# The backward pass of an attention block with a gated MLP: TensorE in program order in the late stages, the w_down gradient among the dh tiles, a hold on the first O^T load, and moved query-stage loads

## The chip, the cores and the metric

The kernel runs on one core of a Trainium2 chip. The metric is the device time of one execution in microseconds (us), lower is better.

## The reference, cut to what matters

```python
def _fwd_reference(A_x, A_k_cache, A_v_cache, A_wq, A_wo, B_x, B_w_gate, B_w_up, B_w_down):
    xn = _layernorm(A_x)                     # [2048, 576], bf16
    s  = attention(xn, k_cache, v_cache, wq) @ wo     # 32 heads of 128, 2048 keys
    g  = silu((sigmoid(xn @ w_gate) * (xn @ w_up)) @ w_down)   # F = 4608
    return A_x + s * g
# the kernel gives this output and the gradients for x, K, V, wq, wo, w_gate, w_up, w_down
```

The order of work in the kernel: layer norm and gated MLP forward; then a long attention loop over 32 heads (to about 3530 us); then the *late stages* that this case is about. They are the O^T stage (attention's output times w_o, the gradient `doB` that enters the MLP, and its transpose `doBT`), 18 MLP blocks of 256 features (gradients of w_down, w_up, w_gate and their part of dx), and the query stage, 8 groups of 4 heads (gradients of w_q and w_o, the rest of dx, and the end of the layer-norm backward in groups 6 and 7). The attention loop writes O and dq to memory; the late stages read them back, and turn them by crossbar transposes (DMA_TRANSPOSE on the queue of SP). In what follows a *turn* is one such transpose, a *jam* is a stretch in which turns take several times their usual issue time, a *pair* is the two matmuls of 512 and 64 columns, dp is the matmul of dO with V^T in attention, and dST are the turned score gradients, sixteen slabs a head.

## The kernel before: the parts that the change and the argument touch

The accumulation of one weight-gradient tile over 16 row tiles, as pairs of matmuls of 512 and 64 columns:

```python
        def accumulate(acc, lhs, rhs, cols, dst):
            for st in range(NT):                       # NT = 16
                for n0, nn in ncs:                     # (0, 512), (512, 64)
                    nc.tensor.matmul(acc[:, n0:n0 + nn], lhsT=lhs[:, st, cols], rhs=rhs[:, st, n0:n0 + nn],
                                     start=(st == 0), stop=(st == NT - 1))
            alt.copy(dst[:, :D], acc[:, :D], eng="s")
```

One MLP block. `dh` has two PSUM buffers, `acc` three:

```python
                for st in range(0, NT, G2):            # G2 = 2: eight dh tiles
                    dh = ps.tile([P, G2, FB], f32, name="dh")
                    ...                                # 10 matmuls of 256 columns
                    nc.vector.tensor_tensor(du_blk[:, sp_, :], dh[:], a_blk[:, sp_, :], op=ALU.mult)
                    nc.scalar.mul(ndh[:], dh[:], -1.0)
                    nc.vector.tensor_tensor(dg_blk[:, sp_, :], ndh[:], nbl[:, sp_, :], op=ALU.mult)
                    if e % NTQ == 0:                   # after each half: crossbar turns of du and dg
                        for k in range(2):
                            turn_rows(dugT[k], dug[k], e - NTQ, e, FBT)
                ...
                if fb == NFB - 1:
                    nc.gpsimd.dma_start(ds_all, rows_view(ds_d, 0, D))    # 2.3 MB
                for fl in range(FBT):                  # w_down gradient, 2 x 16 pairs
                    dwd = outp.tile([P, D], bf, name="dwd")
                    accumulate(psa.tile(...), h_blk, doB, slice(fl * P, (fl + 1) * P), dwd)
                    nc.gpsimd.dma_start(out_8[r0:r0 + P, :], dwd[:])
                ...                                    # w_up, w_gate: 4 x 16 pairs
                for st in range(NT):                   # dx rows: 16 x 4 pairs, need duT and dgT
                    dx_row(acc, st, ...)
```

The late stages are traced in program order for SP, Pool and VectorE; TensorE and ScalarE are ordered by the compiler's scheduler. In the attention loop all engines are. The query stage loads each group's data at the group before (`load_on`, `load_dq`), turns dq (`dqbT`), and in group 6 also turns half of group 7's dq (`dqbT2`), so that rows can be finished there.

## Time and profile before

Three runs before the change gave a median of 4979.05 us (4975.73 to 4979.33). How to read: "start us, us, engine, line, operation, out<-in, count", and in brackets the idle time just before on that engine and what ended it. In lines of SPq the second number is issue time, for which the queue is held. The stages, as differences of first-matmul starts in TensorE's timeline:

| stage | from | us |
|---|---|---|
| attention's end: last head's first dp to first O^T matmul | 3463.86 | 69.4 |
| O^T stage, to the first dh | 3533.30 | 148.7 |
| MLP block 0 | 3681.99 | 49.1 |
| MLP blocks 1 to 16 | 3731.11 | 788.9 |
| MLP block 17 | 4520.01 | 56.2 |
| query group 0 | 4576.18 | 53.6 |
| groups 1 to 5 | 4629.76 | 235.2 |
| group 6 | 4864.96 | 64.6 |
| group 7 to the end of the span | 4929.58 | 51.7 |

VectorE's timeline of the kernel before in one MLP block shows the chain behind a dh tile: du, a wait for ScalarE's ndh, dg, and only then the next du. Its period is 1.75 us.

```profile
3781.71 0.69 DVE L1101 TENSOR_TENSOR du_blk<-dh,ah 128x512 bf16<-128x512 f32 x1 [0.34 <-PE dh L1098]
3783.12 0.43 DVE L1104 TENSOR_TENSOR dg_blk<-ndh,nbl 128x512 bf16<-128x512 bf16 x1 [0.72 <-ACT ndh L1103]
3783.47 0.68 DVE L1101 TENSOR_TENSOR du_blk<-dh,ah 128x512 bf16<-128x512 f32 x1
```

TensorE's timeline has two more waits, in query groups 0 and 6:

```profile
4612.41 17.51 PE L1052 MATMUL acc<-wdT,dqbT 128*128 128x512 bf16 x126 [4.71 <-ACT dqT L40]
...
4886.69 2.10 PE L1052 MATMUL acc<-wqT,dqbT 128*128 128x512 bf16 x8 [4.90 <-DMA dqbT<-dqb]
```

The first is a jam of crossbar turns: ScalarE's copy waits for the turn of an older one. The second is the turn of `dqbT2`, which the first finished row needs.

### The profile page before, as it was taken

The numbers are of one execution on the slowest core, as the hardware profiler recorded it, in microseconds if no ns is written. First come the engines' busy times: TensorE is split into PE (matmuls) and PEld (weight loads), VectorE is DVE, ScalarE is ACT, GpSimd is POOL, SyncE is SP. The second block draws the span as 40 slices with busy tenths as digits, with TensorE's granted clock in tenths as the row PEclk, the third lists the DMA queues.
The fourth block names the chain that finished last, engine by engine and source line by source line (L and its number), as shares of the span: only waits on it lengthen the run. The fifth ranks groups of instructions, "written<-read, shape, count | busy, mean of one in ns | idle before, by whom it ended". The sixth has DMA issues, their size and how long they took to land.

```text
span 4981.3 us, 100870 instructions
## 1 busy us (share of the span) xinstructions
PE 4857.5 (98%) x40276; PEld 2897.3 (58%) x41029; DVE 2790.1 (56%) x6554; ACT 2473.1 (50%) x4228; POOL 840.7 (17%) x1330
## 2 busy tenths in 40 slices
PE   9999999999999999999999999999899999999998
PEld 4445666666666666666666666665455555555454
DVE  4544665666666566566566666666334545453225
ACT  4422766766766766666676676676221111111111
POOL 3322111111111111111111111111221111111111
PEclk9999999999999999999999999999999999999999
DMA  7887999999999999999999999999999999998765
GB/s 260 273 204 173 224 229 225 226 233 228 225 229 221 229 227 225 228 232 230 224 225 237 222 231 226 230 225 224 206 224 235 230 212 228 214 222 160 207 167 146
DMA packets 3048180, 1097.68 MB, mean 220 GB/s; under 512 B 2951889, under 2 KB 2956114, under 8 KB 3047698
## 3 DMA queue, kind: packets, MB, share of 16 engines
q1 hardware_dynamic: 2948930, 771.66, 82.5%
q0 software_dynamic: 98160, 318.85, 20.3%
q8 instruction: 322, 5.28, 0.4%
q14 instruction: 160, 1.31, 0.1%
q10 hardware_dynamic: 608, 0.59, 0.0%
HBM read 175.31 MB, written 177.93 MB: 71 GB/s over the span
## 4 chain that ended last, share of the span: by engine, by line
PE 88%; DVE 4%; issue 3%; DMA 3%; ACT 2%; SPq 1%; POOL 0%; ACTq 0%; POOLq 0%; DVEq 0%
PE acc L683 18%; PE acc L744 17%; PE acc L997 11%; PE sp L636 8%; PE dp L706 8%; PE acc L1052 8%; PE acc L215 6%; PE u_ps L450 3%; PE g_ps L448 3%; PE acc L533 3%; PE acc L957 2%; DVE du_blk L1101 1%; ACT ndh L1103 1%; PE acct L145 1%; DMA dST<-Pq 1%
## 5 line engine op out<-in xcount | busy, mean ns | idle before, releaser
L654 ACT ACTIVATE Pq<-sp 128x1024 bf16<-128x1024 f32 x1024 | 1046.9, 1023 | 262.3 <-PE sp L636 219.2
L709 DVE SCALAR_TENSOR_TENSOR Pq<-dp,negdelta,Pq 128x1024 bf16<-128x1024 f32 x512 | 654.8, 1279 | 46.8 <-PE dp L706 46.6
L712 ACT ACTIVATE t<-dp,negdelta 128x1024 bf16<-128x1024 f32 x512 | 567.1, 1114 | 214.9 <-PE dp L706 165.0
L683 PEld LDWEIGHTS <-dST 128*128 128x128 bf16 x8192 | 508.3, 98 | 157.4 <-DMA dST<-Pq 16.9
L706 PE MATMUL dp<-VT,dOT 128*128 128x512 bf16 x1919 | 581.6, 379 | 2.3
L683 PEld LDWEIGHTS <-PT 128*128 128x128 bf16 x8192 | 500.1, 98 | 128.7 <-DMA PT<-Pq 8.6
L683 PE MATMUL acc<-Kn,dST 128*128 128x128 bf16 x8192 | 557.5, 219 | 13.6 <-DMA dST<-Pq 11.7
L636 PE MATMUL sp<-KQ 128*128 128x512 bf16 x1858 | 567.8, 379 | 2.2 <-ACT Pq L654 2.1
L683 PE MATMUL acc<-Vn,PT 128*128 128x128 bf16 x8192 | 542.1, 219 | 6.4 <-DMA PT<-Pq 4.4
L744 PE MATMUL acc<-Pq,dOn 128*128 128x512 bf16 x1983 | 527.8, 379 | 10.2 <-issue 0.2
L713 DVE TENSOR_TENSOR Pq<-t,Pq 128x1024 bf16<-128x1024 bf16 x512 | 354.4, 692 | 321.1 <-ACT t L712 306.3
L744 PE MATMUL acc<-Pq,Qn 128*128 128x512 bf16 x2013 | 523.7, 379 | 4.9
L1142 DVE TENSOR_TENSOR dxn<-acc,dxn 128x576 f32<-128x576 f32 x272 | 206.0, 757 | 316.9 <-PE acc L1052 316.9
L724 ACT ACTIVATE dq_n<-acc,rsc 128x128 bf16<-128x128 f32 x512 | 187.5, 366 | 339.4 <-PE acc L683 317.9
L744 PEld LDWEIGHTS <-Qn 128*128 128x128 bf16 x2048 | 200.3, 98 | 240.9 <-issue 1.6
L744 PEld LDWEIGHTS <-dOn 128*128 128x128 bf16 x2048 | 199.0, 98 | 234.6 <-issue 1.3
L1103 ACT ACTIVATE ndh<-dh 128x512 bf16<-128x512 f32 x144 | 86.0, 597 | 420.0 <-DVE du_blk L1101 419.9
L636 PEld LDWEIGHTS <-KQ 128*128 128x128 bf16 x2048 | 179.0, 98 | 123.8 <-issue 3.1
L706 PEld LDWEIGHTS <-dOT 128*128 128x128 bf16 x2048 | 178.8, 98 | 124.1 <-issue 11.7
L641 DVE TENSOR_REDUCE rs_all<-rsp 128x1 f32<-128x2 f32 x512 | 78.4, 153 | 306.5 <-ACT Pq L654 295.3
L677 POOL DMA_DIRECT2D on_d<-o_n x128 | 97.1, 759 | 778.7 <-DVE junk L695 458.9
L677 POOL DMA_DIRECT2D dq_d<-dq_n x128 | 97.9, 765 | 721.8 <-ACT dq_n L724 682.0
(209 smaller groups left out, 6800.1 us busy)
## 6 DMA issues: line engine op xcount, KB each, us to landing
out_dram<-kvn POOLq DMA_DIRECT2D x64, 512.0 KB, 3.9
ah<-a_d POOLq DMA_DIRECT2D x18, 1024.0 KB, 9.0
ah<-h_d POOLq DMA_DIRECT2D x18, 1024.0 KB, 10.8
h_d<-h_row POOLq DMA_DIRECT2D x64, 256.0 KB, 3.5
a_d<-a_row POOLq DMA_DIRECT2D x64, 256.0 KB, 3.8
x_all<-in_A_k_cache_dram SPq DMA_DIRECT2D x64, 256.0 KB, 3.8
on_d<-o_n POOLq DMA_DIRECT2D x128, 128.0 KB, 4.6
kvT_d<-KQ POOLq DMA_DIRECT2D x32, 512.0 KB, 5.4
```

Of the source, the lines that this page charges most:

```text
L215: nc.tensor.matmul(av[:, :CH], lhsT=w[:, i, :], rhs=srcT[:, i, cs], start=(i == 0), stop=(i == DT - 1))
L636: nc.tensor.matmul(sp[:, c * CH:(c + 1) * CH], lhsT=hs.QT[:, qt * P:(qt + 1) * P], rhs=hs.KT[:, hf * HW_ + c * CH: hf * HW_ + (c + 1) * CH ...
L654: nc.scalar.activation(Pq[:, hsl], sp[:], AF.Exp, scale=SCALE, accum_out=hs.rsp[:, hf:hf + 1])
L683: nc.tensor.matmul(hs.acc[:, 0, :], lhsT=T[:, kt, :], rhs=rhs[:, kt, :], start=(kt == 0), stop=(kt == NT - 1))
L706: nc.tensor.matmul(dp[:, c * CH:(c + 1) * CH], lhsT=hs.dOT[:, qt * P:(qt + 1) * P], rhs=hs.VT[:, hf * HW_ + c * CH: hf * HW_ + (c + 1) * C ...
L709: nc.vector.scalar_tensor_tensor(Pq[:, hsl], dp[:], hs.negdelta[:, qt:qt + 1], Pq[:, hsl], op0=ALU.add, op1=ALU.mult)
L712: nc.scalar.activation(t[:], dp[:], AF.Identity, bias=hs.negdelta[:, qt:qt + 1], scale=1.0)
L713: nc.vector.tensor_tensor(Pq[:, hsl], t[:], Pq[:, hsl], op=ALU.mult)
L744: nc.tensor.matmul(self.acc, lhsT=self.nat[:, qt, :], rhs=self.slabs[qt][:, cs], start=(qt == self.lo), stop=(qt == self.hi - 1))
L997: nc.tensor.matmul(acc[:, n0:n0 + nn], lhsT=lhs[:, st, cols], rhs=rhs[:, st, n0:n0 + nn], start=(st == 0), stop=(st == NT - 1))
L1052: nc.tensor.matmul(acc[:, n0:n0 + nn], lhsT=lT, rhs=w[:, n0:n0 + nn], start=(k == 0), stop=(k == len(terms) - 1))
L1142: nc.vector.tensor_tensor(dxn[:, st, :], acc[:, :D], dxn[:, st, :], op=ALU.add)
```

## The change

Its intent: (1) TensorE too follows program order in the late stages, and the w_down gradient's 32 pairs are written into the dh loop, four after each dh tile; (2) the first O^T load, 1 MB through the crossbar, is held back by a one-element copy that reads the fifteenth score-gradient slab, so that it can't stand among that head's turns; (3) in the query stage a group's data are loaded two groups ahead, right after the last use of the buffer, the turn of `dqbT2` moves behind the second head of group 6, and the finished rows begin after 5 steps instead of 4.

```diff
-            put(bl + NT, 0, lambda: load_oT(oTs[0], 0))
+            def first_oT():
+                g = max(0, NT - 2)
+                nc.gpsimd.tensor_copy(oTs[0][0:1, 0, 0:1], heads[H - 1].slabs[g][0:1, 0:1])
+                load_oT(oTs[0], 0)
+            put(bl + NT, 0, first_oT)
@@ late stages
-            tc.manual_schedule(engines={... SP, ... Pool, ... DVE}):
+            tc.manual_schedule(engines={... SP, ... Pool, ... DVE, ... PE}):
@@ MLP block
+                def dwd_unit():            # one row tile (a pair); store after the sixteenth
+                    ...
                     nc.vector.tensor_tensor(dg_blk[:, sp_, :], ndh[:], nbl[:, sp_, :], op=ALU.mult)
+                    for _ in range(FBT * G2):          # 4
+                        dwd_unit()
...
-                for fl in range(FBT):
-                    ... accumulate(...); store
+                while dwd_units:
+                    dwd_unit()
@@ query stage
+            if NHG > 1:
+                load_on(onqs[1][0], 1)
+                load_dq(onqs[1][1], 1)
...
-                if not final:
-                    load_on(onqs[(hg + 1) % 2][0], hg + 1)
-                    load_dq(onqs[(hg + 1) % 2][1], hg + 1)
...
-                if early:
-                    nc.sync.dma_start_transpose(wqT2[:], A_wq[:, (hg + 1) * HC:(hg + 2) * HC])
-                    turn_rows(dqbT2, onqs[(hg + 1) % 2][1], 0, NTE, HG)
...
-                wait_n = min(4 if early else 2, nsteps - 2)
+                wait_n = min(5 if early else 2, nsteps - 2)
...                                                    # in the head loop, after the head's dwq turn
+                    if early and hl == min(1, HG - 1):
+                        nc.sync.dma_start_transpose(wqT2[:], ...); turn_rows(dqbT2, ...)
...                                                    # after the head loop
+                    if hg + 2 < NHG:
+                        load_on(onb, hg + 2)
+                        load_dq(dqb, hg + 2)
```

More of the change, by code (lines that the diff above doesn't have):

```diff
@@ L882 @@
     with late("pc") as pc, late("pcf") as pcf, \
-            tc.manual_schedule(engines={mybir.EngineType.SP, mybir.EngineType.Pool, mybir.EngineType.DVE}):
+            tc.manual_schedule(engines={mybir.EngineType.SP, mybir.EngineType.Pool, mybir.EngineType.DVE, mybir.EngineType.PE}):
         xn_all = pc.tile([P, NT, D], bf, name="xn_all")
@@ L992, with accumulate @@
         px.release()
-        def accumulate(acc, lhs, rhs, cols, dst):
-            for st in range(NT):
+        def accumulate(acc, lhs, rhs, cols, dst, a=0, b=NT):
+            for st in range(a, b):
                 for n0, nn in ncs:
@@ L998, in accumulate @@
                                      start=(st == 0), stop=(st == NT - 1))
-            alt.copy(dst[:, :D], acc[:, :D], eng="s")
+            if b == NT:
+                alt.copy(dst[:, :D], acc[:, :D], eng="s")
         def store_T(out_, cols, stg_):
@@ L1089 @@
                 du_blk, dg_blk = dug
+                dwd_units = [(fl, st) for fl in range(FBT) for st in range(NT)]
+                dwd_box = []
+                def dwd_unit():
+                    fl, st = dwd_units.pop(0)
+                    if st == 0:
+                        dwd_box[:] = [outp.tile([P, D], bf, name="dwd"), psa.tile([P, WD], f32, name="acc", tag="acc")]
+                    accumulate(dwd_box[1], h_blk, doB, slice(fl * P, (fl + 1) * P), dwd_box[0], st, st + 1)
+                    if st == NT - 1:
+                        r0 = fb * FB + fl * P
+                        nc.gpsimd.dma_start(out_8[r0:r0 + P, :], dwd_box[0][:])
                 for st in range(0, NT, G2):
@@ L1115 @@
                     nc.gpsimd.dma_start(ds_all, rows_view(ds_d, 0, D))
-                for fl in range(FBT):
-                    dwd = outp.tile([P, D], bf, name="dwd")
-                    accumulate(psa.tile([P, WD], f32, name="acc", tag="acc"), h_blk, doB, slice(fl * P, (fl + 1) * P), dwd)
-                    r0 = fb * FB + fl * P
-                    nc.gpsimd.dma_start(out_8[r0:r0 + P, :], dwd[:])
+                while dwd_units:
+                    dwd_unit()
                 if fb == NFB - 1:
@@ L1227 @@
                     nc.sync.dma_start_transpose(dwq[:, :, lcols], dqTs[h % 2][:])
+                    if early and hl == min(1, HG - 1):
+                        nc.sync.dma_start_transpose(wqT2[:], A_wq[:, (hg + 1) * HC:(hg + 2) * HC])
+                        turn_rows(dqbT2, onqs[(hg + 1) % 2][1], 0, NTE, HG)
                     if final and hl == HG - 1:
```

## The prediction

> **What bounds the kernel now.** I read the page first, then the busy time by 100 us windows from the end of attention on, then TensorE's timeline at every dip, and last the SP queue's timeline and the chain of waits there. The change touches nothing before about 3500 us but one load, so only the last third can move.
>
> ```profile
> PE 4857.5 (98%) x40276; PEld 2897.3 (58%) x41029; DVE 2790.1 (56%) x6554; ACT 2473.1 (50%) x4228; POOL 840.7 (17%) x1330
> ```
> ```profile
> 3400.00:3500.00 100.00, 94.44 (x822) 59.32 (x835) 60.53 (x161) 63.80 (x110) 17.70 (x34) 0.98 1.14 223
> 3500.00:3600.00 100.00, 79.08 (x640) 44.04 (x652) 25.42 (x35) 16.61 (x33) 22.00 (x40) 0.91 0.94 199
> ...
> 3900.00:4000.00 100.00, 98.39 (x800) 56.89 (x813) 50.44 (x80) 17.29 (x29) 16.49 (x24) 1.00 0.95 221
> ...
> 4500.00:4600.00 100.00, 94.60 (x746) 51.56 (x759) 32.52 (x48) 12.32 (x20) 13.60 (x19) 0.97 0.88 166
> 4600.00:4700.00 100.00, 94.50 (x750) 48.67 (x764) 24.23 (x32) 10.65 (x17) 11.70 (x16) 0.98 0.82 204
> 4700.00:4800.00 100.00, 99.17 (x801) 51.45 (x816) 24.24 (x32) 11.48 (x18) 12.23 (x17) 1.00 0.61 177
> 4800.00:4900.00 100.00, 94.15 (x738) 48.64 (x752) 32.09 (x51) 10.56 (x16) 13.83 (x20) 0.97 0.72 196
> ```
> The first figure after the window's length is PE. TensorE is the bound nearly everywhere. From 3500 us it is idle for 67 us in all (1481 us of windows less 1414 us busy), and a part of that is the unavoidable tail. The change keeps every matmul, so its gain is a part of those 67 us plus idle time that busy time hides (some 20 us, below): under 2% of 4979 even if all of it went.
>
> Hidden idle time is in the MLP blocks (18 of them, 3682 to 4576 us). TensorE's timeline in one:
> ```profile
> 3780.42 2.35 PE L1098 MATMUL dh<-wdT,doBT 128*128 128x256 bf16 x20
> 3782.60 0.41 PE L997 MATMUL acc<-doB,ah 128*128 128x512 bf16 x2
> 3783.14 1.25 PE L1098 MATMUL dh<-wdT,doBT 128*128 128x256 bf16 x10
> 3784.23 0.62 PE L997 MATMUL acc<-doB,ah 128*128 128x512 bf16 x3
> 3784.89 1.25 PE L1098 MATMUL dh<-wdT,doBT 128*128 128x256 bf16 x10
> ...
> 3793.19 5.34 PE L997 MATMUL acc<-doB,ah 128*128 128x64 bf16 x43
> 3798.36 8.00 PE L997 MATMUL acc<-xn_all,du_blk 128*128 128x512 bf16 x62
> 3806.20 8.00 PE L997 MATMUL acc<-xn_all,dg_blk 128*128 128x512 bf16 x63
> ```
> So the scheduler already puts some w_down-gradient matmuls (doB, ah) between dh tiles, but only one or two pairs each, and two thirds of them stand in a lump after the last dh. dh tiles start every 1.75 us although a tile and two pairs need less: the next tile waits for its PSUM buffer.
>
> The two places where the crossbar queue stops TensorE, SP's queue first (issue time), then TensorE with its wait:
> ```profile
> 3502.77 4.93 SPq L584 DMA_TRANSPOSE KQ<-on_d  x1
> 3507.79 18.95 SPq L630 DMA_TRANSPOSE dST<-Pq  x8
> ```
> ```profile
> 3513.11 1.57 PE L683 MATMUL acc<-Kn,dST 128*128 128x128 bf16 x16 [4.02 <-DMA dST<-Pq]
> ...
> 4563.72 0.66 PE L1052 MATMUL acc<-wug,duT 128*128 128x512 bf16 x4 [2.08 <-DMA duT<-du_blk]
> 4566.56 0.74 PE L1052 MATMUL acc<-wug,dgT 128*128 128x64 bf16 x3 [2.18 <-DMA dgT<-dg_blk]
> ```
> The O^T load (KQ) holds SP for 4.93 us in the middle of sixteen score-gradient turns; the ninth comes late and TensorE waits 4.02 us. In the last MLP block the second half of dgT comes 25.6 us after its issue.
>
> **What the Trainium skill says.** (1) "TensorE: Matmul & The Clock Gate", section "Wait — 56ns, not 53.3ns?": back-to-back warm matmuls start N/2.4 GHz plus about 2.5 ns apart. That makes 109.2 ns for 256 columns and 215.8 + 29.2 = 245 ns for a 512 and 64 pair. The trace agrees: ten dh matmuls in 1.09 us (3783.14 to 3784.23), 32 pairs in 7.84 us (3798.36 to 3806.20). (2) Same page, "What's actually happening": after an idle window the clock is halved for some 3.4 us. The trace agrees: after the 4566 wait the four-matmul steps start 0.96 us apart for about 4.8 us, then 0.49. (3) "Perfetto Trace Analysis", "Tensor Engine Instruction": the end of a matmul is estimated. So I go by starts, not by busy time; it is why a 49.3 us block shows under 1 us idle.
>
> **The change, part by part.**
>
> (a) w_down gradient among dh, blocks 1 to 16. Floor of a block: 80 dh matmuls x 0.1092 = 8.7 us; w_down, w_up, w_gate gradients 32 pairs each and dx 64 pairs, 160 x 0.245 = 39.2 us; sum 47.9. Period now: (4520.01 - 3780.42) / 15 = 49.31. Loss 1.4 us. Its cause is the chain behind dh: VectorE du 0.68, ScalarE ndh 0.60, VectorE dg 0.42 and hand-overs, 1.75 us a tile, which is just the pitch seen. The change puts four pairs after each tile: 1.09 + 0.98 = 2.07 us of TensorE work, above 1.75, so the PSUM wait should be gone. All 32 pairs are then used up, so no lump. What follows (w_up) has du ready except the last slice, and 4 pairs stand between. Gain 1.4 x 16 = 22 us. TensorE in program order by itself costs nothing here, since the order seen is the program's but for these pairs.
>
> (b) Block 0. There VectorE also makes nbl (0.6), pitch about 2.35 us. Now the scheduler fills with up to four pairs and even w_up's. In program order 2.07 us of work meets 2.35: eight tiles lose up to 0.28 each. Loss about 1.5 us against now (49.1 us).
>
> (c) Block 17. It takes 4576.18 - 4520.01 = 56.2 us, 8.3 above the floor: 1.4 as in (a), 4.3 the two waits, about 2.4 the cold clock (five steps of 0.96 for 0.49). Cause: the 2.3 MB ds load is issued at 4532.93, just after the last dh and just before the second-half turns (4534.27 and 4540.47). In the change the Pool queue meets the two w_down-gradient stores first, and the second comes only when all dh and pairs are done plus the 0.64 copy: about 17.5 us into the block, estimate from the times above. The du turn is then issued at about 16.3 and the dg turn at 17 to 18, at or ahead of the ds load instead of behind. They are needed at 16.4 + 15.7 + 7.8 = 40 us. I expect both waits to go; 7 of 8.3 us, with one of doubt.
>
> (d) First O^T load. SP's turns take about 2.4 us each (18.95 / 8) and 4.93 go to O^T. Taking it out brings turns 9 to 16 forward by 4.9, so the 4.02 wait goes and with it about 2 us of cold clock. Against: if the queue places the load before the last turn, that turn is no earlier than now; and the load now arrives later. It is wanted when O^T matmuls begin (3533.3), and even then those take 6 us and TensorE then idles 10.5 us for w_o rows, which follow Pool's stores at the end of attention; so a late landing up to some 10 us costs nothing. The chain behind moves with attention's end. Gain 5 us, between 0 and 7.
>
> (e) Query stage. Eight groups; groups 1 to 5 start 47.04 us apart, exactly 192 pairs x 0.245, so nothing to gain. Group 0 loses 4.7 us and cold clock behind crossbar turns of 32.6 us issue time beside 4 MB of loads; the same loads are issued at about the same place: 0, plus or minus 4. Group 6 (4864.96 to 4929.58, 64.6 us) loses 4.9 us at the dqbT2 turn, which lands 21.7 us after the start. The change moves that turn behind the second head's: about 12.4 (third step plus copy), two short turns, w_q 2.2, then 6.8 as now: 24 us, for a row that begins at 19.6 + 1. The wait becomes some 3.5, but VectorE's rows (4.36 us each, 8 rows, 34.9) start at 25 instead of 24 and are what ends last: 25 + 35 + 8 x 0.69 = 65.8. So 0, plus or minus 2. The earlier loads for the group after next gain nothing: Pool already ran ahead and issued them at 4852.7. The last group keeps its 52 us.
>
> Sum: 22 - 1.5 + 7 + 5 + 0 = 32.5. Predicted 4979 - 32 = 4947 us.
>
> **Rivals.** R1: the pitch of dh isn't set by the chain to be overtaken, or four pairs make a new wait (the accumulator's copy on ScalarE between ndh, or later dg turns reaching dx late). For it: the slack between last dg and its use shrinks from about 27 to 23 us, DMA is 0.95 busy. Against: turns land in 4.0 us median in these blocks. Then (a) gives nothing: about 4967. R2: program order costs more than it saves where the scheduler filled (block 0, first O^T rows, group 6): some 10 us back, about 4957. R3: (c) moves the DMA jam instead of removing it: ds, on and the next loads, 2 MB each, then collide with the group 0 turns, which lengthen 4.7 to 10; about 4953. R4: everything works and group 0 and 6 give 3 to 5 each: 4938.
>
> **Range and chances.** (a) is counted sixteen times and rests on starts, so most weight lies within 10 us of 4947. The rivals are mostly on the slow side: 4937 to 4962. Faster by 2% would need 100 us, more than all idle time in these stages; slower by 2% would need 5 us a block everywhere. 0.01, 0.98, 0.01.
>
> **What would show it.** Period of dh starts 47.9 to 48.2 in blocks 1 to 16, dh tiles 2.07 us apart with eight other matmuls between; block 0 about 50.5; block 17 about 49 with no wait for dgT; no 4 us dST wait before the last O^T load and its issue after at least the fifteenth turn; group 6 at 63 to 67 us. A period still at 49.3 would make the prediction wrong, as would a new wait at dx rows 8 to 15 or an O^T load that lands after the w_o rows.

## The result, and the profile after

The changed kernel took 4962.84 us in the median of 4 runs (4958.1 to 4968.66), against 4977.39 for the kernel before (4 runs, 4973.89 to 4979.33). A ratio here is the mean time of one kernel's fast runs over that of the other's of the same rounds, so not quite the ratio of the medians that are quoted: 0.9972, 95% interval 0.9955 to 0.9989. That is a gain of 14.5 us by the medians where 32 were forecast; 4962.84 lies just above the range of 4937 to 4962.

TensorE's line of the changed kernel's page, then its busy time by 100 us windows (after the window's length: PE, PEld, DVE, ACT, POOL; then clock, DMA share, GB/s):

```profile
PE 4881.5 (98%) x41029; PEld 2895.9 (58%) x41029; DVE 2801.3 (56%) x6554; ACT 2474.6 (50%) x4228; POOL 842.3 (17%) x1331
```
```profile
3500.00:3600.00 100.00, 73.58 (x614) 42.77 (x613) 27.89 (x35) 19.99 (x36) 19.23 (x35) 0.86 0.93 187
...
3900.00:4000.00 100.00, 100.00 (x838) 58.95 (x837) 54.07 (x84) 18.50 (x32) 17.09 (x25) 1.00 1.04 224
...
4500.00:4600.00 100.00, 100.00 (x827) 54.76 (x826) 36.97 (x53) 13.51 (x22) 17.00 (x23) 1.00 0.76 202
4600.00:4700.00 100.00, 100.00 (x818) 51.41 (x817) 28.81 (x39) 10.22 (x16) 11.68 (x16) 1.00 0.69 200
...
4800.00:4900.00 100.00, 95.07 (x755) 48.40 (x754) 32.89 (x67) 15.04 (x22) 14.76 (x25) 0.97 0.65 159
```

The MLP blocks and the first query groups are now full. The hole in front of them, at 3500 to 3600 us, is 26 us here and was 21 in the first profile of before, but the stages begin 11 us later here, so the window does not hold the same work. (Some TensorE records were missing in the trace of before, 40276 of 41029; so the busy time of the page is not a fair comparison, and starts are.)

One MLP block in TensorE's timeline:

```profile
3747.71 1.26 PE L1115 MATMUL dh<-wdT,doBT 128*128 128x256 bf16 x10
3748.81 1.14 PE L1002 MATMUL acc<-doB,ah 128*128 128x512 bf16 x8
3749.79 1.26 PE L1115 MATMUL dh<-wdT,doBT 128*128 128x256 bf16 x10
...
3762.22 1.26 PE L1115 MATMUL dh<-wdT,doBT 128*128 128x256 bf16 x10
3763.31 1.14 PE L1002 MATMUL acc<-doB,ah 128*128 128x512 bf16 x8
3764.29 6.01 PE L1002 MATMUL acc<-xn_all,du_blk 128*128 128x512 bf16 x47
```

dh tiles start 2.07 us apart with eight other matmuls between, and nothing waits. Now the end of attention and the start of the O^T stage, SP's queue and then TensorE:

```profile
3486.68 39.47 SPq L630 DMA_TRANSPOSE dST<-Pq  x14
3526.32 5.12 SPq L584 DMA_TRANSPOSE KQ<-on_d  x1
3531.53 4.23 SPq L630 DMA_TRANSPOSE dST<-Pq  x2
3551.39 5.00 SPq L584 DMA_TRANSPOSE xnT<-on_d  x1
```
```profile
3536.00 1.89 PE L683 MATMUL acc<-Kn,dST 128*128 128x128 bf16 x16 [5.41 <-DMA dST<-Pq]
...
3570.12 6.87 PE L962 MATMUL acc<-dsT,xnT 128*128 128x512 bf16 x34 [19.47 <-DMA xnT<-on_d]
```

The O^T load now stands in front of the last two turns instead of in the middle of sixteen, and the wait went with it: 5.41 us at the fifteenth turn where it had been 4.02 at the ninth. The last line shows a larger one, which no edit here was aimed at: in the O^T stage TensorE waits for the second O^T load or for rows of w_o, 19.47 us at a stretch in this profile, 7.5 to 21.1 in the longest such wait of each of the fourteen. And group 6, SP's queue and then TensorE:

```profile
4848.90 9.14 SPq L1053 DMA_TRANSPOSE dqbT<-ah  x4
4858.27 2.52 SPq L1240 DMA_TRANSPOSE dwq<-dqT  x2
4860.83 3.26 SPq L1242 DMA_TRANSPOSE wqT<-in_A_wq_dram  x1
4864.20 4.24 SPq L1053 DMA_TRANSPOSE dqbT<-dqb  x1
```
```profile
4870.49 2.10 PE L1058 MATMUL acc<-wqT,dqbT 128*128 128x512 bf16 x8 [4.93 <-DMA dqbT<-dqb]
...
4908.34 6.52 PE L1058 MATMUL acc<-wdT,dqbT 128*128 128x512 bf16 x32 [3.21 <-DVE dxn L1261]
```

The group begins at 4844.82. Its first row still waits 4.93 us for `dqbT2`, which now comes 25.7 us after the start instead of 21.7; VectorE's rows follow from there, and TensorE waits for them again at the end (1.34 and 3.21 us). The first ten or so of its last sixteen pairs then start 480 ns apart instead of 245, so that four rows of 4 pairs take 6.4 us where they take 3.92 at full clock.

All stages, with the later profiles of both kernels (experiments below), in us:

| stage | before, three profiles | changed, two profiles |
|---|---|---|
| the last head's first dp starts at | 3463.9, 3465.7, 3463.8 | 3473.2, 3466.6 |
| attention's end | 69.4, 65.5, 72.6 | 71.1, 68.9 |
| O^T stage | 148.7, 153.8, 155.1 | 153.3, 153.8 |
| block 0 | 49.1, 49.1, 49.1 | 50.1, 50.1 |
| blocks 1 to 16 | 788.9, 789.0, 789.1 | 766.9, 766.9 |
| block 17 | 56.2, 52.2, 49.3 | 47.9, 47.9 |
| group 0 | 53.6, 47.0, 47.0 | 47.0, 47.0 |
| groups 1 to 5 | 235.2 in all | 235.2 in both |
| group 6 | 64.6, 64.2, 64.1 | 69.9, 67.9 |
| group 7 to the end | 51.7, 51.9, 51.9 | 52.2, 52.1 |

Two kinds of rows: MLP blocks 0 to 16 and groups 1 to 5 repeat to 0.2 us, attention's end, the O^T stage, block 17 and group 0 vary by 6 to 7 us in the three profiles of before. The first profile of before had the worst jam of the three.

### The profile page after: what moved, and what is told of

It reads as the page before. It is cut to its first block, busy times and chain, and to the rows that moved or that the text cites. A ratio compares the mean times of both kernels' runs of the same rounds, so it can differ in the third digit from the quotient of the medians.

```text
span 4966.9 us, 101629 instructions
## 1 busy us (share of the span) xinstructions
PE 4881.5 (98%) x41029; PEld 2895.9 (58%) x41029; DVE 2801.3 (56%) x6554; ACT 2474.6 (50%) x4228; POOL 842.3 (17%) x1331
## 5 line engine op out<-in xcount | busy, mean ns | idle before, releaser
L706 PE MATMUL dp<-VT,dOT 128*128 128x512 bf16 x2048 | 609.7, 379 | 2.2
L636 PE MATMUL sp<-KQ 128*128 128x512 bf16 x2048 | 609.5, 379 | 2.2 <-ACT Pq L654 2.1
```

The costliest lines, as they stand in the source:

```text
L636: nc.tensor.matmul(sp[:, c * CH:(c + 1) * CH], lhsT=hs.QT[:, qt * P:(qt + 1) * P], rhs=hs.KT[:, hf * HW_ + c * CH: hf * HW_ + (c + 1) * CH ...
L706: nc.tensor.matmul(dp[:, c * CH:(c + 1) * CH], lhsT=hs.dOT[:, qt * P:(qt + 1) * P], rhs=hs.VT[:, hf * HW_ + c * CH: hf * HW_ + (c + 1) * C ...
```

## The experiments

Twelve kernels ran, in three calls on three chips (1, 11 and 12; for the first result the record names no chip), so ratios of one call compare best. Runs of the kernel before had medians of 4978.20, 4977.49 and 4978.16 us and spread from 4960 to 4986. All gave a correct result. The stages of the ones that follow, in us, from TensorE's timeline as above:

| run | median us | ratio to before, 95% interval | attention's end | O^T | block 17 | group 0 | group 6 |
|---|---|---|---|---|---|---|---|
| e1_same (changed, again) | 4955.93 | 0.9958 (0.994 to 0.9977) | 68.9 | 153.8 | 47.9 | 47.0 | 67.9 |
| e2_no_hold | 4954.42 | 0.9957 (0.9937 to 0.9976) | 66.4 | 147.2 | 47.9 | 47.0 | 70.5 |
| e3_hold_only | 4976.61 | 1.0003 (0.9986 to 1.0021) | 68.0 | 146.2 | 53.0 | 47.0 | 63.5 |
| e4_old_query | 4950.94 | 0.9951 (0.9933 to 0.9969) | 66.8 | 148.4 | 47.9 | 55.2 | 62.9 |
| e5_order_only | 5028.58 | 1.0093 (1.0071 to 1.0115) | 71.3 | 152.4 | 51.8 | 47.0 | 64.6 |
| e7_ds_late | 4975.47 | 0.9987 (0.9969 to 1.0005) | 67.0 | 154.9 | 49.3 | 47.0 | 64.4 |
| e9_hold_last | 4955.95 | 0.9945 (0.9921 to 0.9969) | 64.4 | 142.7 | 47.9 | 47.0 | 69.5 |
| e6_among_only | 4956.02 | 0.9955 (0.9942 to 0.9968) | 62.2 | 150.3 | 48.2 | 54.9 | 63.2 |
| e10_early_turn | 4949.65 | 0.9944 (0.993 to 0.9958) | 65.6 | 153.9 | 48.2 | 46.8 | 56.6 |
| e11_both | 4941.82 | 0.9926 (0.9913 to 0.994) | 63.8 | 151.8 | 47.9 | 47.0 | 56.7 |

### How far one profile repeats: the two kernels again

No edit in either. The changed kernel:

> The changed kernel unedited, for a second profile. In the first pair of profiles the last head's first dp matmul came at 3473.2 us against 3463.9 before, although the instruction order up to there is the same. Theory A (run to run noise of the attention loop): that start moves by some 5 us or more either way in this profile, and the stages from the first O^T matmul on repeat to within 2 us: O^T stage 153, MLP blocks 1 to 16 767, block 17 48, group 0 47.0, group 6 70 us. Theory B (the change slows attention itself): dp starts again at 3473 or later. Gain over before 14 us in either.

The kernel before, two more times:

> The kernel before, unedited, profiled a second time. Theory A (the first profile of before fell on a bad jam): block 17 plus group 0 take clearly less than the 109.7 us of the first profile, near the 100.0 that the hold-only run showed with the same code there. Theory B (the jam is the same each run): 109 to 110. Blocks 1 to 16 at 789 in both.

> The kernel before, a third profile. Block 17 plus group 0 at 99 to 101 if the 109.7 of the first profile was the exception, near 110 if the second was.

Measured: 4955.93 us in the median of 6 runs for the changed kernel; with the first four, ten runs between 4947.5 and 4968.7, mean 4958. The dp matmul that had come at 3473.2 us now came at 3466.6, and over all fourteen profiles it lies between 3463.8 and 3477.4 with the same instructions in the same order up to there. So the 9 us by which the first changed profile was late at that point are noise of the attention loop, not an effect of the change: theory A. Block 17 and group 0 of before took 109.7, 99.2 and 96.4 us together in three profiles of one and the same kernel. The wait for dgT in the second one, and SP's queue in the third, where the turn took 14 us of issue time and still came in time:

```profile
4567.88 0.66 PE L1052 MATMUL acc<-wug,dgT 128*128 128x512 bf16 x4 [2.66 <-DMA dgT<-dg_blk]
```
```profile
4544.00 5.88 SPq L1047 DMA_TRANSPOSE duT<-du_blk  x1
4549.97 14.05 SPq L1047 DMA_TRANSPOSE dgT<-dg_blk  x1
```

My forecast of block 17 and my reading of group 0 rested on the worst of the three. (The forecast for the third, 99 to 101 or 110, missed too: it was 96.4, lower than both.)

### The interleaving or the order

```diff
-            tc.manual_schedule(engines={SP, Pool, DVE}):
+            tc.manual_schedule(engines={SP, Pool, DVE, PE}):      # nothing else, on the kernel before
```

> The kernel before with TensorE put in program order and nothing else, so all 32 w_down pairs of a block stand after its eight dh tiles. Theory A (the interleaving is what gains, the order alone doesn't): dh tiles at their chain's pitch of 1.75 us with nothing between, so a block of about 8 x 1.75 + 152 pairs... that is 14 us of dh plus 160 x 0.245 = 39.2, about 53 us; blocks 1 to 16 about 850 us, 60 slower than before. Theory B (program order itself is the gain): 767 us. One more sample of block 17 and group 0 with the ds load in its old place.

Measured: 5028.58 us, 51 slower than before; blocks 1 to 16 took 828.2 us, 51.8 each. TensorE's timeline in one block:

```profile
4529.25 1.25 PE L1098 MATMUL dh<-wdT,doBT 128*128 128x256 bf16 x10 [0.38 <-ACT ndh L1103]
4531.00 1.25 PE L1098 MATMUL dh<-wdT,doBT 128*128 128x256 bf16 x10 [0.50 <-ACT ndh L1103]
4532.75 1.25 PE L1098 MATMUL dh<-wdT,doBT 128*128 128x256 bf16 x10 [0.50 <-ACT ndh L1103]
...
4539.09 8.00 PE L997 MATMUL acc<-doB,ah 128*128 128x512 bf16 x64
```

With nothing to put between, dh tiles start 1.75 us apart, the period of the chain in VectorE's timeline, and TensorE waits each time for ScalarE's ndh, which frees the PSUM buffer. A block of 51.8 us is less than the 53 that I expected: with two buffers only six of the eight tiles wait, and 6 x (1.75 - 1.09) makes 4.0 us; measured are 3.9 over the floor of 47.9. So program order alone loses what the scheduler's own partial interleaving had gained, and the four pairs after each tile are what gains. Not run was the opposite, the pairs written there and TensorE left to the scheduler; whether program order is needed beside them is not shown.

### That part alone

The changed kernel without the hold and with its query stage as before:

```diff
-            put(bl + NT, 0, first_oT)
+            put(bl + NT, 0, lambda: load_oT(oTs[0], 0))
@@ query stage: loads, dqbT2 turn and wait_n = 4 as in the kernel before
```

> Program order with w_down among dh alone: no hold, query stage as before. If the gain of the change is this part and the rest nets to nothing: as fast as or a little faster than the changed kernel (4950 to 4957), blocks 1 to 16 at 767, block 17 at 48, group 6 at 63 to 65, group 0 at 47 or, if its jam comes, 53 to 55. If hold and query edits were needed for the gain: slower than the changed kernel by over 5.

Measured: 4956.02 us, ratio 0.9955 (0.9942 to 0.9968); the changed kernel had 0.9958 in its own call. Blocks 1 to 16 took 766.9. So this part gives the whole gain, and the hold and the query edits net to nothing that these runs can tell. Group 0 jammed, though.

### The query edits

Only the query stage put back:

```diff
+                if not final:
+                    load_on(onqs[(hg + 1) % 2][0], hg + 1)
+                    load_dq(onqs[(hg + 1) % 2][1], hg + 1)
+                if early:
+                    (wqT2 and dqbT2 turns here)
-                (loads two groups ahead; turns behind the second head)
-                wait_n = min(5 if early else 2, nsteps - 2)
+                wait_n = min(4 if early else 2, nsteps - 2)
```

> The changed kernel with its query stage put back (loads, the place of the second dqbT turn, wait of 4 steps). Theory A (the later turn of dqbT2 costs, and the stall of group 0 went with the jam in block 17): group 6 back at about 64.6 us from 69.9, group 0 still 47.0; 5 us faster than the changed kernel. Theory B (the earlier loads freed group 0): group 0 back at 53, so total about 1 us slower.

Measured: 4950.94 us, not told apart from the changed kernel (0.9951 against 0.9958, intervals overlap). Of each theory one stage came true. Group 6 went back to 62.9 us, so the later turn, with rows from the fifth step, costs 5 to 7. Group 0 went to 55.2. Its jam in this run: the Pool queue, SP's queue, TensorE's busy time and DMA (last two columns: share, GB/s) in its first 10 us:

```profile
4546.47 1.19 POOL L1032 DMA_DIRECT2D onb<-on_d  x1
4547.66 1.16 POOL L1035 DMA_DIRECT2D dqb<-dq_d  x1
```
```profile
4549.54 24.16 SPq L1053 DMA_TRANSPOSE dqbT<-ah  x1
```
```profile
4550.00:4560.00 10.00, 10.00 (x85) 5.16 (x83) 0.00 (x0) 1.53 (x3) 0.57 (x1) 1.00 1.33 44
```

Two loads of 2 MB are issued 1.2 us apart just when the turns begin, and one turn takes 24.16 us of issue time. The DMA engines are busy throughout; they move 44 GB/s in the first 10 us, 216 and 333 in the next two stretches of 10. With the query code as changed, the second load waits 5 to 6 us for TensorE's last dx row (in all six such profiles; with the old code too in four of eight, 3.1 to 8.2 us), and group 0 took 47.0 us or less in six of six; with the old query code behind a block 17 of 48 us it took 55.2 and 54.9 in two of two.

That the query edit is the reason is not shown, and the traces speak against it. Up to and past these two loads and the four turns, Pool and SP issue the same transfers in the same order in all eight of these kernels: the edit changes what comes later. The delay of e4 and e6 begins before any query code, in block 17:

```profile
4519.43 12.61 SPq L1147 DMA_TRANSPOSE dwu<-dwT  x2
```

These two turns took 12.61 us in e4 and 11.57 in e6, and 3.23 to 5.17 in the other six. So the stores behind them came late, and the loads behind the stores came late and together. Why is open; the place of tiles in memory, which the edit may move, and chance were not told apart. Nor do two close loads always jam: in e8 and e3 they were issued 1.5 us apart as the turns began, and group 0 took 47.0. The first profile of before jammed (53.6) although its second load did wait. So the query edit pays 5 us or more in group 6, and what it buys in group 0 is open.

### The ds load in front of the last turns

The kernel before, its 2.3 MB ds load issued after the w_down gradient's stores:

```diff
-                if fb == NFB - 1:
-                    nc.gpsimd.dma_start(ds_all, rows_view(ds_d, 0, D))
                 for fl in range(FBT):
                     ...                                # w_down gradient, store
+                if fb == NFB - 1:
+                    nc.gpsimd.dma_start(ds_all, rows_view(ds_d, 0, D))
```

> The kernel before with the 2.3 MB ds load issued behind the two w_down-gradient stores of the last block instead of just after its last dh. Theory A (the load in front of the second-half turns is what jams block 17): no wait for duT or dgT, block 17 about 49.5 us against 56.2 in the first profile; blocks 1 to 16 stay at 789. Theory B (the jam comes from the later loads, or varies from run to run): waits of a few us remain.

Measured: block 17 at 49.3 us, no wait for duT or dgT, and SP's queue is free:

```profile
4551.77 1.42 SPq L1047 DMA_TRANSPOSE duT<-du_blk  x1
4553.28 3.19 SPq L1047 DMA_TRANSPOSE dgT<-dg_blk  x1
```

So with the load behind the turns the jam was gone (3.19 us for the dgT turn here; 14.05 to 20.42 in the three profiles of before and in e3), as forecast. It is not the whole story, though. e5 has the load in front, and its dgT turn took 7.67 us. And in e2 and e10, kernels with the changed order, the turn was issued half a us before the load and still took 13.87 and 13.28 us, where it took 3.61 to 4.09 in the six others with that order. SP's queue and Pool's in e2:

```profile
4519.97 13.87 SPq L1048 DMA_TRANSPOSE dgT<-dg_blk  x1
```
```profile
4520.46 1.17 POOL L1129 DMA_DIRECT2D doBT<-ds_d  x1
```

It still came in time, issued 18.0 us into the block against 20.2 to 20.9 in before. By the time of the whole kernel e7 is not told apart from before (0.9987, interval 0.9969 to 1.0005), as is fitting for a jam that costs 0 to 7 us.

### The hold

The changed kernel without it (edit as in the first diff of "That part alone"):

> The changed kernel without the hold on the first O^T load, all else kept. Theory A (the hold costs, since it moves the 4.9 us load in front of the last two score-gradient turns and shifts the O^T stage's loads): about 6 us faster than the changed kernel, with attention's end 69.4 us after the last head's first dp, a 4 us wait at the ninth turn, and an O^T stage of 149 us. Theory B (my forecast, the hold gains 5): 5 us slower. Theory C (the late O^T stage comes from TensorE's program order and not from the hold): attention's end gets better, the O^T stage stays at 153.

The kernel before with it:

> The kernel before with nothing but the hold. Theory A: 4 to 8 us slower than before (4983), the wait moved from the ninth to the fifteenth turn. Theory B (forecast): 5 us faster (4972). Theory C (program order is to blame): end of attention 1 to 2 us later only, O^T stage as before at 149 us.

Neither theory of these two held. e2 and e1 ran with 0.9957 and 0.9958; e3 has 1.0003. The wait of TensorE sits at the ninth turn without the hold (4.02, 3.64 and 3.55 us in before, e8 and e2) and at the fifteenth with it (5.41, 3.61, 6.03, 5.46 and 5.93 in the changed kernel, e1, e3, e4 and e10). Attention's end and O^T stage together take 214 to 224 us with the hold (five profiles) and 213 to 228 without (seven). The 4.7 us by which the O^T stage was longer in the first pair of profiles (153.3 against 148.7), which I had put down to the hold, lie within this spread. Nor is TensorE's program order to blame in the O^T stage: e3, with the scheduler's order, and e2, with program order, take 146 and 147 us.

Then the load behind all sixteen turns:

```diff
-                g = max(0, NT - 2)
-                nc.gpsimd.tensor_copy(oTs[0][0:1, 0, 0:1], heads[H - 1].slabs[g][0:1, 0:1])
+                nc.gpsimd.tensor_copy(oTs[0][0:1, 0, 0:1], heads[H - 1].slabs[NT - 1][0:1, S - 1:S])
```

> The changed kernel with the hold tied to the last column of the last slab, so that the O^T load stands behind all sixteen turns in the queue (seen in its instruction order). Theory A (the load's 4.9 us in front of two turns is the new wait): the 3.6 to 6 us wait at the fifteenth turn goes, attention ends 64 to 66 us after the first dp against 67 to 71, and the O^T stage is not longer, since its start waits for other loads. Theory B: the late load makes the O^T matmuls wait and the sum of the two stages stays at 215 to 224.

Measured: SP's queue and TensorE:

```profile
3491.59 40.31 SPq L630 DMA_TRANSPOSE dST<-Pq  x16
3532.07 4.80 SPq L584 DMA_TRANSPOSE KQ<-on_d  x1
```
```profile
3541.04 5.97 PE L961 MATMUL acc<-dsT,KQ 128*128 128x512 bf16 x34 [3.31 <-DMA KQ<-on_d]
```

No wait for a score-gradient turn is left in e9; in e11, with the same hold, two of 1.51 and 1.44 us are. The O^T matmuls wait 3.31 us for their load, but the O^T stage, whose length hangs on later loads, took 142.7. Attention's end and O^T stage together: 207.1 us here and 215.6 in e11, against 214 to 224 with the hold as changed. By time (0.9945) it is not told apart from the changed kernel (0.9958), since the intervals overlap; the direction fits the forecast, but with one short O^T stage in e9 and one of usual length in e11 (151.8) a gain is not shown.

### The turn before group 6

The turn of `dqbT2` put before group 6, behind group 5's own turns, with dq loaded before on, and rows from the third step:

```diff
                     if hg + 2 < NHG:
-                        load_on(onb, hg + 2)
                         load_dq(dqb, hg + 2)
+                        load_on(onb, hg + 2)
+                    if hg + 2 == NHG - 1:
+                        nc.sync.dma_start_transpose(wqT2[:], A_wq[:, (hg + 2) * HC:(hg + 3) * HC])
+                        turn_rows(dqbT2, dqb, 0, NTE, HG)
...
-                wait_n = min(5 if early else 2, nsteps - 2)
+                wait_n = min(3 if early else 2, nsteps - 2)
```

> The changed kernel with the second dqbT turn (and its w_q part) put before group 6, behind group 5's head turns, its data loaded first, and rows begun after 3 steps. If group 6 is long because its first row waits for this turn and VectorE's 35 us of rows follow it: group 6 at 55 to 57 us from 68 to 70, no wait for dqbT, 12 us faster than the changed kernel. If VectorE alone is what ends it: 62 or more.

> Early turn and the hold behind all sixteen turns together. If the two are independent: attention's end 64 to 66, O^T stage 143 to 150, group 6 at 55 to 57; total about 4935 to 4940, the fastest of all.

Group 6 fell to 56.6 and 56.7 us (its 224 pairs x 0.245 are 54.9). The only wait left in it in e10:

```profile
4846.34 1.15 PE L1058 MATMUL acc<-wdT,dqbT 128*128 128x512 bf16 x8 [1.56 <-DMA dqbT<-ah]
```

So group 6 was long because its rows began late, not because VectorE's 35 us of rows can't be hidden. (The turn, the order of the loads and the third step were changed together.) e10 took 4949.65 us, by time not told apart from the changed kernel. e11, with the hold behind all turns, took 4941.82 us; ratio 0.9926 (0.9913 to 0.994), 36 us under before by the medians and the fastest of all. Its interval lies below that of the changed kernel's first result and just meets that of e1 (0.994 to 0.9977). A little above the 4935 to 4940 that I expected.

## Why the prediction was wrong, point by point

- **Blocks 1 to 16, step (a)**: held to the decimal. 47.93 us a block against a floor of 47.9; gain 22.0 us against 22. dh pitch 2.07 us, no wait. e5 shows the chain of 1.75 us as the cause. Rival R1 fell. "TensorE in program order by itself costs nothing here" was wrong taken alone: in e5 it costs 39 us over these sixteen blocks. The pairs make up for it.
- **Block 0, step (b)**: loss 0.95 us against 1.5; right in kind, a little smaller.
- **Block 17, step (c)**: both waits went, in all eight profiles with the changed order, and e7 fits the mechanism, the ds load in front of the turns, with the limits said there. The size was off: the excess over 47.9 is 8.3, 4.2 and 1.4 us in three profiles of before, mean 4.6, where the forecast took 7 from the worst of them.
- **First O^T load, step (d)**: this step failed. "Taking it out brings turns 9 to 16 forward by 4.9, so the 4.02 wait goes" is true of the ninth turn; but the load of about 5 us stayed ahead of the last two, and the wait came back at the fifteenth with 3.6 to 6.0 us. The gain was 0 within a noise of some 5 us, where 5 had been put into the sum. The text had named this as what speaks against, and then given it too little weight: the load went from behind the eighth turn to behind the fourteenth (not "at least the fifteenth"), so the queue's work ahead of the last two stayed the same. In e9, behind the last turn, the wait is gone; in e11 1.5 us are left.
- **Query stage, step (e)**: the second failure. For group 6 the term was 65.8 - 64.6, taken as 0 (its own sum, 25 + 35 + 8 x 0.69, makes 65.5), and measured 68 to 70.5. Two sizes were off. The turn landed 25.7 us after the start instead of 24 (24.3 to 26.8 in four profiles): the four dqbT turns and the two short ones held SP until 16 us after the start. And the tail was counted at VectorE's 0.69 us a row, while the last four rows go at TensorE's pace: 0.98 us a row at full clock, and 1.6 here, where most of their pairs ran at half pace after a 3.21 us wait. For group 0 "0, plus or minus 4" held as far as is known: its 2.2 us in the means come from the one bad profile of before. In e4 and e6 the jam that R3 had feared did come, 8 us; whether the query edit keeps it away is not shown.
- **Sum**: by stage means of the table, -22.0 (blocks 1 to 16), +0.95 (block 0), -4.6 (block 17), -2.2 (group 0), +4.6 (group 6), +0.4 (group 7) and about +2 within the noise of attention's end and the O^T stage give -21 us. The forecast was -32: (d), forecast at 5 gained, came out at about 2 lost, which is 7 of the difference and within the noise; group 6 is some 5, block 17 2.4, and group 0 and block 0 give back 2 to 3. The ratio's interval, 0.9955 to 0.9989, means a gain of 5 to 22 us, so -14.5 and this -21 don't contradict each other: the ten runs of the changed kernel average 4958, 19 under before's 4977. Single runs spread by 26 us in the kernel before, as much as the width of the forecast's range.

## What to carry to other kernels

Where matmuls wait for a PSUM buffer that a chain on other engines frees, compare the chain's period with the work that can stand between two of them, and write just enough independent matmuls there; the floor from instruction counts then forecast the block here to a tenth of a microsecond. A transfer that was moved back in SP's queue moved the wait along with it; ask which turns it still stands in front of. And before a wait of a few microseconds in a DMA jam is put into a sum, profile the same kernel again: here the same jam cost 0 to 7 us. Before a jam is put down to an edit, look for the first transfer that came late: here it stood before the edited code.

## What the Trainium skill lacked or had wrong

- "DMA: Bandwidth & Descriptors", section "DMA Transpose (X-bar)", does not say how much a crossbar turn slows beside large loads. The dgT turn of 0.5 MB took 3.19 to 4.09 us of issue time in seven of the nine profiles with the 2.3 MB load issued after it and 13.28 and 13.87 in two, 7.67 to 20.42 in the five with the load in front, and a dqbT turn 24.16 us beside two loads of 2 MB, in whose first 10 us the busy DMA engines moved 44 GB/s.
- "TensorE: Matmul & The Clock Gate", section "What's actually happening", gives some 3.4 us at half clock after an idle window and speaks of a free-running window; one such stretch here lasted about 4.7 us (after the wait at 4566 us of the kernel before), and the waits before it were 2.08 and 2.18 us. The prediction's "the trace agrees" is true of the halving, not of its length. The figure for the spacing of warm matmuls in the section "Wait — 56ns, not 53.3ns?" held: 245 ns for a pair of 512 and 64 columns.
- "Perfetto Trace Analysis" does not say how far waits repeat from profile to profile. Here TensorE-bound stages repeat to 0.2 us and those with waits for DMA vary by 6 to 7 us, with 4960 to 4986 us for whole runs of one kernel.
